# Tail keys read in place, weights fetched in odd units, first x tiles on another queue, pools that wait by tile

## Chip, cores, metric

The kernel runs on one core of one Trainium2 chip. The metric is the device time of one execution in microseconds (us). Before the change the median was 2362.5 us (3 runs, 2361.6 to 2363.9).

## The reference

Four layers in the order A, B, A, B on 2048 tokens of 640 numbers, each on the layer norm of its input, with a residual sum. (The norms and the sums are in the part that is cut here.)

```python
def _A_ref(x, wq, wk, wv, wo, beta):          # 32 heads of 20, 4 segments of 512 tokens
    ...
    for s in range(4):
        logits = einsum('bhqd,bhkd->bhqk', qs, ks) * scale + mask     # causal
        a_dot = softmax(logits) @ vs
        num, den = phi(qs) @ M, phi(qs) @ z + 1e-6                    # memory of earlier segments
        outs.append(g * num / den + (1 - g) * a_dot)
        M, z = M + phi(ks)^T vs, z + sum(phi(ks))
    return o @ wo

def _B_ref(x, mem0, Wq, Wk, Wv, Wo, seg_len): # 32 heads of 128, 64 steps of 32 tokens
    mem = mem0                                # 8 memory tokens
    for s in range(64):
        h = concatenate([mem, xs])            # 8 + 32 rows
        q, k, v = h Wq, h Wk, h Wv
        p = softmax(where(mask, q k^T * scale, -1e9))
        o = (p v) Wo
        mem = o[:8]                           # the next step needs it
        outs.append(o[8:])
```

## The kernel before

Layer A works in 32 units (4 segments times 8 groups of four heads). Each unit ends in one VectorE addition called `a_r`, so the distance from one `a_r` to the next is the time of a unit. Layer B does 64 dependent steps. Of a step's 32 tokens, 24 are put through with the 8 memory tokens; the last 8 (the "tail") of four steps are projected together in advance (`b_QTt`, `b_KTt`, `b_Vtb`) and each step takes its own 8 of them.

The first A layer also fetches the projection weights of B, 15 portions of 1 MB (four loads each), one per unit:

```python
xts = [ln_load(0, tt, "a_xt" if tt < 2 else "a_xr") for tt in range(4)]  # SyncE's queue (SP)
fill_pads = prep() if prep else None    # q and k weights of A, ScalarE's queue (ACT)
load_vo(A_wv)                           # a_wvo, 800 KB, SP
# ... cut
for u in range(NU + 1):
    if u + 2 < NU:
        wload(u + 2)                    # a_wt: two loads per unit
    if pre and u >= 1:
        pre.pop(0)()                    # 1 MB of B's weights
```

In B the tail's keys are copied into the step's key tile (GpSimd) and its values are loaded into another tile (DMA), so that the second score and value matmuls (`k = 1`) can use 8 columns or rows of them:

```python
def tails_to_seg(s):
    T, i = divmod(s, 4)
    nc.gpsimd.tensor_copy(heads(QT[s])[:, :, 32:40], QTt[T][:, :, 8 * i:8 * i + 8])
    nc.gpsimd.tensor_copy(heads(KT[s])[:, :, 32:40], KTt[T][:, :, 8 * i:8 * i + 8])
    for j in range(4):
        nc.sync.dma_start(Vt[s][32 * j:32 * j + 8, :, :],
                          Vtb[T][32 * j + 8 * i:32 * j + 8 * i + 8, :, :])
# ... cut: scores
for k, n in ((0, 32), (1, 8)):
    for j in range(4):
        nc.tensor.matmul(o, lhsT=KT[s][:, 40 * h + 32 * k:40 * h + 32 * k + n], ...)
```

The start of a B layer asks for its first x tile, for 5 MB of output weights, and for the second x tile. It builds the mask there too:

```python
ln_dma(0)                               # b_xt, 160 KB
nc.sync.dma_start(m0[:, 0, :], mem0)
for q in range(4):                      # b_wo, 4 x 1280 KB
    nc_raw.sync.dma_start(W.wo[:, 8 * q:8 * q + 8, :], wo_src[:, 8 * q:8 * q + 8, :])
ln_dma(1)                               # b_xt, the second
ln_norm(0); ln_apply(0); ln_tr(0)
# ... cut: b_blk and b_mask built; tails and first queries and keys
ln_norm(1); ln_apply(1)                 # waits for the second b_xt, on VectorE
```

Names in the profiles below: in A, `a_st` are the layer-norm statistics of an x tile, `a_VP` and `a_PP` are projections on TensorE and `a_KN` the keys transposed by it. In B, `b_Qa` is the first projection of a step's queries, `b_Kb` the last one of its keys, `b_TQ` their transposition on VectorE, and `b_OPSd` the output projection of the tails.

Memory of a pool that closes is given to the pools that open after it; by default the first users of that memory wait for all that the closed pool's users in the region had outstanding.

## Time and profile before

| what | before |
|---|---|
| median of 3 runs | 2362.5 us |
| TensorE (PE) busy | 2226.6 of 2364.3 us (94%) |
| four steady steps of B | 52.4 us |
| the two B layers, `b_Qa` to the last `b_OPSd` | about 1680 us |
| first A layer, first to last `a_r` | 266.4 us |
| second A layer, the same | 259.6 us |

Three lines of the profile's page of the kernel before. The second has each engine's busy time, its share of the span and its instructions. In the third each digit is a fortieth of the span: the busy share of the DMA engines in tenths.

```profile
span 2364.3 us, 123472 instructions
PE 2226.6 (94%) x54988; PEld 1242.1 (53%) x54988; DVE 1578.4 (67%) x3636; ACT 949.3 (40%) x2207; POOL 1073.2 (45%) x2603
DMA  6773341111111111110033333400000001000000
```

TensorE is busy for 94% of the span. The DMA engines are busy in the A layers and nearly idle in B. The first A layer (about five digits) starts with 67733: bunched.

The windows view of before. Columns: stretch (us), its length, then busy time of each engine with the number of instructions, granted clock (the share of full speed at which TensorE's clock ran), DMA share, GB/s.

```profile
core 0: us, PE busy (x) PEld busy (x) DVE busy (x) ACT busy (x) POOL busy (x), PEclk, DMA share, GB/s
96.00:144.00 48.00, 39.34 (x413) 20.53 (x412) 31.02 (x80) 28.23 (x41) 20.18 (x49) 0.89 0.96 235
442.92:495.34 52.42, 52.20 (x1534) 29.54 (x1534) 35.97 (x79) 16.74 (x51) 25.70 (x62) 1.00 0.11 25
```

In 96 to 144 us the DMA engines are at 0.96 and TensorE is idle 8.7 of 48 us. In the steady B stretch of the last line TensorE is busy 52.20 of 52.42 us at full clock: it waits for 0.22 us, so relieving another engine can gain next to nothing there.

The chain of waits of before between 85 and 142 us (start, length, what was waited for): the work that ended last was held up by transfers.

```profile
88.16 7.28 DMA a_wt<-a_wpad
...
106.39 4.55 DMA a_wt<-a_wpad
...
110.96 5.92 DMA a_xt<-in_A_x_dram
...
128.94 10.22 DMA a_xt<-in_A_x_dram
```

```profile
1491.44 0.89 DVE L85 BATCH_NORM_STATS2 b_ln_st<-b_xt 128x6 f32<-128x320 bf16 x2 [2.65 <-DMA xres<-a_xr]
...
1511.30 0.85 DVE L85 BATCH_NORM_STATS2 b_ln_st<-b_xt 128x6 f32<-128x320 bf16 x2
```

```profile
1510.36 1.27 PE L85 MATMUL b_Qa<-b_wq,b_hT 128*32 128x512 bf16 x20
...
1514.38 0.61 PE L85 MATMUL b_Kb<-b_wk,b_hT 128*32 128x512 bf16 x8 [0.59 <-DVE b_TQ L85]
```

B's first statistics at 1491.44 waited 2.65 us for a store of layer A. The second x tile is asked for behind the four b_wo loads; its statistics at 1511.30 show no wait, and b_Kb starts at 1514.38 after a wait of 0.59.

The start of before, all engines; in brackets stands the idle time of the engine before the instruction, and what ended it:

```profile
0.81 2.15 SPq L215 DMA_DIRECT2D a_xt<-in_A_x_dram  x4
...
1.32 0.55 ACTq L143 DMA_DIRECT2D b_wv<-in_A_wk_dram  x1
...
3.00 0.74 SPq L198 DMA_DIRECT2D a_wvo<-in_A_wv_dram  x1
...
7.03 0.89 DVE L85 BATCH_NORM_STATS2 a_st<-a_xt 128x6 f32<-128x320 bf16 x2 [1.36 <-DMA a_xt<-in_A_x_dram]
...
16.06 0.95 ACT L85 COPY b_wv<-b_wv 128x400 bf16<-128x400 bf16 x2
```

Three value groups in a row on TensorE in before, two of 8 rows and one of 32. Each group is four matmuls, on four separate 32-row strips of the array. The groups start 25 ns apart in the median, behind one that streams 40 columns and behind one that streams 16 alike:

```profile
1519.29 0.17 PE L85 MATMUL b_OTL<-b_PT,b_Vt 8*128 8x16 bf16 x4
1519.32 0.18 PE L85 MATMUL b_OTL<-b_PT,b_Vsb 32*128 32x40 bf16 x4
1519.34 0.17 PE L85 MATMUL b_OTL<-b_PT,b_Vt 8*128 8x16 bf16 x4
```

### The profile page before, as it was taken

The page shows a single profiled execution, that of the slowest core. Times are in us where ns is not written, and L with a number is a line of the kernel's source. Part 1 is how long each engine was busy: PE and PEld are TensorE (multiplying, and loading weights), DVE is VectorE, ACT ScalarE, POOL GpSimd, SP SyncE. Part 2 cuts the span into 40 slices and gives each one's busy share as a digit, 9 for nine tenths or more (in the row PEclk, how much of TensorE's full clock was granted, in tenths as well). Part 3 has the DMA queues.
Part 4 walks back from the last instruction along what each step waited for, and adds up shares of the span by engine and source line. Part 5 has one row for each costly group of instructions (what it writes and reads, how often), then busy time and mean ns, then how long its engine had stood idle before and what let it go on. Part 6 is the DMA issues. An engine that isn't in the chain of part 4 may idle for free.

```text
span 2364.3 us, 123472 instructions
## 1 busy us (share of the span) xinstructions
PE 2226.6 (94%) x54988; PEld 1242.1 (53%) x54988; DVE 1578.4 (67%) x3636; ACT 949.3 (40%) x2207; POOL 1073.2 (45%) x2603
## 2 busy tenths in 40 slices
PE   7989979999999999999879998799999999999997
PEld 3444435555555555555545444455555555555554
DVE  6677646666666666666667776466666666666665
ACT  5666723332323233323257767133232323332322
POOL 3344434454454444544323444345445445444442
PEclk9999989999999999999989999899999999999999
DMA  6773341111111111110033333400000001000000
GB/s 173 196 184 99 107 143 24 26 23 26 24 24 23 25 26 26 23 24 21 21 115 109 107 108 109 151 22 23 20 22 20 22 22 23 22 23 21 19 18 16
DMA packets 98847, 131.83 MB, mean 56 GB/s; under 512 B 20592, under 2 KB 84096, under 8 KB 96384
## 3 DMA queue, kind: packets, MB, share of 16 engines
q1 hardware_dynamic: 96992, 122.21, 19.1%
q8 instruction: 431, 7.06, 1.3%
q10 hardware_dynamic: 1312, 1.64, 0.2%
q14 instruction: 112, 0.92, 0.1%
HBM read 89.17 MB, written 26.21 MB: 49 GB/s over the span
## 4 chain that ended last, share of the span: by engine, by line
PE 79%; DVE 10%; ACT 4%; issue 2%; DMA 2%; POOL 1%; SPq 0%; DVEq 0%; POOLq 0%; ACTq 0%
PE b_OPS L85 13%; PE b_V L85 12%; PE b_tail L85 7%; PE b_Qa L85 7%; PE b_Kb L85 6%; PE b_Qb L85 6%; PE b_Ka L85 6%; PE b_SP L85 4%; PE a_PP L85 4%; PE b_OTL L85 3%; ACT a_PT L85 3%; PE b_OPSd L85 3%; PE a_S L85 2%; PE a_pv L85 2%; DVE b_TM L85 1%
## 5 line engine op out<-in xcount | busy, mean ns | idle before, releaser
L85 PEld LDWEIGHTS <-b_hT 128*32 128x32 bf16 x15520 | 379.9, 96 | 339.5 <-DVE b_hT L85 65.8
L85 ACT ACTIVATE b_PT<-b_SP 128x224 bf16<-128x224 f32 x256 | 92.2, 360 | 773.1 <-DVE b_TQ L85 731.1
L85 PE MATMUL b_V<-b_wv,b_hT 128*32 128x512 bf16 x5120 | 361.5, 381 | 0.0
L85 ACT ACTIVATE a_PT<-a_S 128x768 bf16<-128x768 f32 (+1 forms) x384 | 326.5, 892 | 67.4 <-PE a_S L85 57.0
L85 PE MATMUL b_OPS<-b_wo,b_OTsb 128*32 128x320 bf16 x8192 | 325.9, 300 | 5.9 <-DVE b_OTsb L85 5.1
L85 PEld LDWEIGHTS <-b_OTsb 128*32 128x32 bf16 x8192 | 195.1, 96 | 114.2 <-DVE b_OTsb L85 49.5
L85 POOL CAST b_QT<-b_TQ 128x384 bf16<-128x384 f32 x254 | 140.8, 554 | 238.5 <-DVE b_TQ L85 238.5
L85 ACT CAST b_OTsb<-b_OTL 128x320 bf16<-128x320 f32 x384 | 150.9, 428 | 228.3 <-PE b_OTL L85 200.3
L85 POOL CAST b_KT<-b_TQ 128x384 bf16<-128x384 f32 x254 | 142.5, 561 | 162.4 <-DVE b_TQ L85 161.2
L85 POOL TENSOR_TENSOR b_PT<-b_PT,b_R 128x64 bf16<-128x64 bf16 x256 | 105.1, 411 | 216.4 <-ACT b_R L85 191.9
L85 POOL TENSOR_SCALAR_AFFINE_SELECT a_PT<-a_PT 128x256 bf16<-128x256 bf16 x256 | 107.8, 422 | 199.3 <-ACT a_PT L85 188.1
L85 PE MATMUL b_Kb<-b_wk,b_hT 128*32 128x512 bf16 x2560 | 185.5, 381 | 1.2 <-DVE b_TQ L85 1.2
L85 PE MATMUL b_Qa<-b_wq,b_hT 128*32 128x512 bf16 x2560 | 161.7, 381 | 13.4 <-DVE b_hT L85 7.1
L85 PE MATMUL b_Qb<-b_wq,b_hT 128*32 128x512 bf16 x2560 | 160.4, 379 | 0.0
L85 PE MATMUL b_Ka<-b_wk,b_hT 128*32 128x512 bf16 x2560 | 160.4, 379 | 0.0
L85 PE MATMUL a_PP<-a_xnT,a_wt 128*128 128x512 bf16 x560 | 151.1, 404 | 7.5 <-DVE a_um L85 1.7
L85 PE MATMUL a_S<-a_qk 32*128 32x512 bf16 (+3 forms) x1024 | 138.8, 312 | 8.1 <-ACT a_PT L85 6.4
L85 DVE STREAM_TRANSPOSE b_TM<-b_OPS 128x320 f32<-128x320 f32 x126 | 65.2, 517 | 115.2 <-PE b_OPS L85 115.2
L85 DVE TENSOR_TENSOR b_PT<-b_PT,b_R 128x160 bf16<-128x160 bf16 x256 | 103.5, 404 | 49.4 <-ACT b_R L85 29.5
L85 DVE CAST b_Vsb<-b_V 128x512 bf16<-128x512 f32 x128 | 88.5, 692 | 68.2 <-PE b_SP L85 53.5
L85 DVE STREAM_TRANSPOSE b_TQ<-b_Qa 128x512 f32<-128x512 f32 x128 | 91.7, 716 | 62.5 <-PE b_Qa L85 40.9
L85 DVE CAST b_OTsb<-b_OTL 128x320 bf16<-128x320 f32 x128 | 62.9, 492 | 104.5 <-PE b_OTL L85 104.5
(148 smaller groups left out, 4154.9 us busy)
## 6 DMA issues: line engine op xcount, KB each, us to landing
a_wt<-a_wpad SPq DMA_DIRECT2D x112, 160.0 KB
b_wo<-in_B_Wo_dram SPq DMA_DIRECT2D x8, 1280.0 KB
b_Vt<-b_Vtb SPq DMA_DIRECT2D x512, 16.0 KB
b_XO<-xres SPq DMA_DIRECT2D x256, 30.0 KB
a_wvo<-in_A_wo_dram SPq DMA_DIRECT2D x8, 800.0 KB
b_wq<-in_B_Wq_dram SPq DMA_DIRECT2D x20, 256.0 KB
b_wk<-in_B_Wk_dram SPq DMA_DIRECT2D x20, 256.0 KB
xres<-a_xo SPq DMA_DIRECT2D x16, 320.0 KB
```

Of the source, the lines that this page charges most:

```text
L85: r = f(*a, **k)
```

## The change

1. The tail's keys and values are read where they lie. The second score and value matmuls use all 32 tail keys of the four steps; a mask per step hides 24 of them. The copies to `b_KT` and the `b_Vt` loads go. The masks are built once, in the first A layer ahead of the first `a_qk`, not at each start of B.
2. B's weights are fetched in odd units only, so the 15 MB are spread over twice as many units.
3. The first x tiles of each A layer are issued from ScalarE's queue.
4. All pools of A and B wait by tile: a tile in reused memory waits only for what used its own bytes.

The diff, cut to its core:

```diff
+def build_masks(nc, C):                          # called in the first layer A
+    C.mask = C.pool.tile([128, 4, 40], BF16, name="c_mask")
+    nc.vector.memset(C.mask[:], 0.0)
+    ...                                           # 16 affine_select on GpSimd
+    C.blk = C.pool.tile([128, 4, 32], BF16, name="c_blk")
+    ...                                           # 5 memsets on VectorE
-        st = ctx.enter_context(tc.tile_pool(name="a_state", bufs=1))
+        st = ctx.enter_context(tc.tile_pool(name="a_state", bufs=1, reuse_waits="tile"))
     ...                                           # likewise all pools of A and B
-        xts = [ln_load(0, tt, "a_xt" if tt < 2 else "a_xr") for tt in range(4)]
+        xts = [ln_load(0, tt, "a_xt" if tt < 2 else "a_xr", nc.scalar) for tt in range(4)]
-                if pre and u >= 1:
+                if pre and u % 2:
     ...
-            nc.gpsimd.tensor_copy(heads(KT[s])[:, :, 32:40], KTt[T][:, :, 8 * i:8 * i + 8])
-            for j in range(4):
-                nc.sync.dma_start(Vt[s][32 * j:32 * j + 8, :, :], Vtb[T][32 * j + 8 * i:32 * j + 8 * i + 8, :, :])
-        (b_blk, b_mask built at the start of B)
     ...
-                            nc.tensor.matmul(o, lhsT=KT[s][:, 40 * h + 32 * k:40 * h + 32 * k + n],
+                            nc.tensor.matmul(o, lhsT=KTt[T][:, h, :] if k else KT[s][:, 32 * h:32 * h + 32],
     ...
-                        V_ = Vsb if k == 0 else Vt[s]
+                        V_ = Vtb[T] if k else Vsb
```

More of the change, by code (lines that the diff above doesn't have):

```diff
@@ L103, in __getattr__ @@
         return getattr(self._nc, attr)
+def build_masks(nc, C):
+    if hasattr(C, "mask"):
+        return
+    C.mask = C.pool.tile([128, 4, 40], BF16, name="c_mask")
+    nc.vector.memset(C.mask[:], 0.0)
+    for j in range(4):
+        m = C.mask[32 * j:32 * j + 32]
+        nc.gpsimd.affine_select(out=m[:, :, 0:16], in_=m[:, :, 0:16], pattern=[[-8, 4], [0, 16]], compare_op=ALU.is_ge,
+                                fill=-1e9, base=0, channel_multiplier=1)
+        nc.gpsimd.affine_select(out=m[:, :, 0:8], in_=m[:, :, 0:8], pattern=[[8, 4], [0, 8]], compare_op=ALU.is_ge,
+                                fill=-1e9, base=7, channel_multiplier=-1)
+        nc.gpsimd.affine_select(out=m[:, :, 8:16], in_=m[:, :, 8:16], pattern=[[8, 4], [1, 8]], compare_op=ALU.is_ge,
+                                fill=-1e9, base=0, channel_multiplier=-1)
+        m = C.mask[32 * j:32 * j + 24, :, 16:40]
+        nc.gpsimd.affine_select(out=m, in_=m, pattern=[[0, 4], [1, 24]], compare_op=ALU.is_ge,
+                                fill=-1e9, base=0, channel_multiplier=-1)
+    C.blk = C.pool.tile([128, 4, 32], BF16, name="c_blk")
+    nc.vector.memset(C.blk[:], 0.0)
+    for j in range(4):
+        nc.vector.memset(C.blk[32 * j:32 * j + 32, j, :], 1.0)
 def watch(nc, C, sums, inverses):
@@ L180, in layer_A @@
     with ExitStack() as ctx:
-        st = ctx.enter_context(tc.tile_pool(name="a_state", bufs=1))
-        wk = ctx.enter_context(tc.tile_pool(name="a_wk", bufs=2))
-        wk1 = ctx.enter_context(tc.tile_pool(name="a_wk1", bufs=1))
-        pg = ctx.enter_context(tc.tile_pool(name="a_pg", bufs=2, space=PSUM))
-        pss = ctx.enter_context(tc.tile_pool(name="a_pss", bufs=2, space=PSUM))
-        ppv = ctx.enter_context(tc.tile_pool(name="a_ppv", bufs=1, space=PSUM))
+        st = ctx.enter_context(tc.tile_pool(name="a_state", bufs=1, reuse_waits="tile"))
+        wk = ctx.enter_context(tc.tile_pool(name="a_wk", bufs=2, reuse_waits="tile"))
+        wk1 = ctx.enter_context(tc.tile_pool(name="a_wk1", bufs=1, reuse_waits="tile"))
+        pg = ctx.enter_context(tc.tile_pool(name="a_pg", bufs=2, reuse_waits="tile", space=PSUM))
+        pss = ctx.enter_context(tc.tile_pool(name="a_pss", bufs=2, reuse_waits="tile", space=PSUM))
+        ppv = ctx.enter_context(tc.tile_pool(name="a_ppv", bufs=1, reuse_waits="tile", space=PSUM))
         MZ32 = st.tile([128, NG, 4, 21], F32, name="a_MZ32")
@@ L210, in wload, with ln_load @@
             wts[u] = [wt[:, 0], wt[:, 1]]
-        def ln_load(n, tt, tag="a_xt"):
+        def ln_load(n, tt, tag="a_xt", q=nc_raw.sync):
             r0 = n * 512 + tt * 128
             xt = wk.tile([128, D], xdt, name="a_xt", tag=tag)
-            nc_raw.sync.dma_start(xt[:], x_src[r0:r0 + 128, :])
+            q.dma_start(xt[:], x_src[r0:r0 + 128, :])
             return xt
@@ L283, in layer_A @@
         gg = W.gates(nc, st)
+        build_masks(nc, C)
         def run(gctx):
@@ L287, in run @@
             if general:
-                gp = gctx.enter_context(tc.tile_pool(name="a_gen", bufs=1))
+                gp = gctx.enter_context(tc.tile_pool(name="a_gen", bufs=1, reuse_waits="tile"))
                 negs = wk1.tile([128, 128], F32, name="a_negs", tag="a_xn")
@@ L594, in layer_B @@
     with ExitStack() as ctx:
-        st = ctx.enter_context(tc.tile_pool(name="b_state", bufs=1))
-        wk2 = ctx.enter_context(tc.tile_pool(name="b_wk2", bufs=2))
+        st = ctx.enter_context(tc.tile_pool(name="b_state", bufs=1, reuse_waits="tile"))
+        wk2 = ctx.enter_context(tc.tile_pool(name="b_wk2", bufs=2, reuse_waits="tile"))
         hp = qkp = sm = wk2
         wk = st
-        wop = ctx.enter_context(tc.tile_pool(name="b_wo", bufs=1))
+        wop = ctx.enter_context(tc.tile_pool(name="b_wo", bufs=1, reuse_waits="tile"))
         W.wo = wop.tile([128, 32, D], BF16, name="b_wo")
-        pp = ctx.enter_context(tc.tile_pool(name="b_ps", bufs=3, space=PSUM))
-        po = ctx.enter_context(tc.tile_pool(name="b_po", bufs=1, space=PSUM))
-        pot = ctx.enter_context(tc.tile_pool(name="b_pot", bufs=2, space=PSUM))
+        pp = ctx.enter_context(tc.tile_pool(name="b_ps", bufs=3, reuse_waits="tile", space=PSUM))
+        po = ctx.enter_context(tc.tile_pool(name="b_po", bufs=1, reuse_waits="tile", space=PSUM))
+        pot = ctx.enter_context(tc.tile_pool(name="b_pot", bufs=2, reuse_waits="tile", space=PSUM))
         def ps_tile(shape, dtype, name):
@@ L653, in heads @@
         def heads(t):
-            return t[:, 0:1280].rearrange("p (h c) -> p h c", c=40)
+            return t[:].rearrange("p (h c) -> p h c", h=32)
         def alloc_h(s):
@@ L665, in alloc_qk @@
             QT[s] = qkp.tile([128, 32 * 40], BF16, name="b_QT", tag="QT")
-            KT[s] = qkp.tile([128, 32 * 40], BF16, name="b_KT", tag="KT")
+            KT[s] = qkp.tile([128, 32 * 32], BF16, name="b_KT", tag="KT")
         def w_heads(Wt, c, b, j):
@@ L696, in place @@
             evac(eng, dst3[:, 16 * b:16 * b + 16, c0:c0 + (t1 - t0)], tq[:, :, t0:t1])
-        QTt, KTt, Vtb, Vt = {}, {}, {}, {}
+        QTt, KTt, Vtb = {}, {}, {}
         hx = {}
@@ L755, in tails_to_seg @@
             nc.gpsimd.tensor_copy(heads(QT[s])[:, :, 32:40], QTt[T][:, :, 8 * i:8 * i + 8])
-            nc.gpsimd.tensor_copy(heads(KT[s])[:, :, 32:40], KTt[T][:, :, 8 * i:8 * i + 8])
-            Vt[s] = qkp.tile([128, 2, 512], BF16, name="b_Vt", tag="Vt")
-            for j in range(4):
-                nc.sync.dma_start(Vt[s][32 * j:32 * j + 8, :, :], Vtb[T][32 * j + 8 * i:32 * j + 8 * i + 8, :, :])
         class OPass:
@@ L809, in layer_B @@
             nc.vector.memset(ones[:], 1.0)
-        blk = st.tile([128, 2, 4, 32], BF16, name="b_blk")
-        nc.vector.memset(blk[:], 0.0)
-        for j in range(4):
-            nc.vector.memset(blk[32 * j:32 * j + 32, 0, j, :], 1.0)
-            nc.vector.memset(blk[32 * j:32 * j + 8, 1, j, :], 1.0)
         if not general:
@@ L819, in layer_B @@
         nc.vector.memset(XO[:], 0.0)
-        negs = wk.tile([128, 32], F32, name="b_negs", tag="Vsb")
-        nc.vector.memset(negs[:], -1e9)
-        mask = st.tile([128, 40], BF16, name="b_mask")
-        maskf = wk.tile([128, 40], F32, name="b_maskf", tag="tsc")
-        nc.vector.memset(maskf[:], 0.0)
-        for j in range(4):
-            r0 = 32 * j
-            nc.gpsimd.affine_select(out=maskf[r0:r0 + 24, 16:40], in_=negs[r0:r0 + 24, 0:24],
-                                    pattern=[[-1, 24]], compare_op=ALU.is_gt, fill=0.0, base=0, channel_multiplier=1)
-            nc.gpsimd.affine_select(out=maskf[r0:r0 + 8, 8:16], in_=negs[r0:r0 + 8, 0:8],
-                                    pattern=[[-1, 8]], compare_op=ALU.is_gt, fill=0.0, base=0, channel_multiplier=1)
-        nc.vector.tensor_copy(mask[:], maskf[:])
         if general:
             maskq = st.tile([128, 40], BF16, name="b_maskq")
-            maskqf = wk.tile([128, 40], F32, name="b_maskqf", tag="tsc")
+            maskqf = wk.tile([128, 40], F32, name="b_maskqf", tag="xnb")
+            negs = wk.tile([128, 32], F32, name="b_negs", tag="Vsb")
+            nc.vector.memset(negs[:], -1e9)
             nc.vector.memset(maskqf[:], 0.0)
@@ L922, in row_max @@
                         h = 16 * b + 8 * q + i
-                        nc.tensor.matmul(sp[:, i, :], lhsT=QT[s][:, 40 * h:40 * h + 40], rhs=KT[s][:, 40 * h:40 * h + 40],
+                        nc.tensor.matmul(sp[:, i, 0:32], lhsT=QT[s][:, 40 * h:40 * h + 40], rhs=KT[s][:, 32 * h:32 * h + 32],
+                                         start=False, stop=True, skip_group_check=True)
+                        nc.tensor.matmul(sp[:, i, 32:40], lhsT=QT[s][:, 40 * h:40 * h + 40], rhs=KTt[T][:, h, 8 * i4:8 * i4 + 8],
                                          start=False, stop=True, skip_group_check=True)
@@ L965, in scores @@
                     nc.tensor.matmul(sp[32 * j:32 * j + 32, :, 0:40], lhsT=C.identb[:, 32 * j:32 * j + 32],
-                                     rhs=mask[:].unsqueeze(1).to_broadcast([128, 4, 40]),
+                                     rhs=C.mask[:, i4].unsqueeze(1).to_broadcast([128, 4, 40]),
                                      start=True, stop=False, tile_position=(0, 32 * j), skip_group_check=True)
                 for r in range(4):
-                    for k, n in ((0, 32), (1, 8)):
+                    for k in range(2):
                         for j in range(4):
                             h = 16 * b + 4 * j + r
-                            o = sp[32 * j:32 * j + n, r, 16:56] if k == 0 else sp[32 * j:32 * j + n, r, 0:16]
-                            nc.tensor.matmul(o, lhsT=KT[s][:, 40 * h + 32 * k:40 * h + 32 * k + n],
+                            o = sp[32 * j:32 * j + 32, r, 0:16] if k else sp[32 * j:32 * j + 32, r, 16:56]
+                            nc.tensor.matmul(o, lhsT=KTt[T][:, h, :] if k else KT[s][:, 32 * h:32 * h + 32],
                                              rhs=QT[s][:, 40 * h + 24 * k:40 * h + 40], start=False, stop=True,
@@ L976, in scores @@
                 if general:
-                    for k, n in ((0, 32), (1, 8)):
+                    for k in range(2):
                         for j in range(4):
                             h = 4 * j
-                            o = sp[32 * j:32 * j + n, :, 16:56] if k == 0 else sp[32 * j:32 * j + n, :, 0:16]
-                            nc.tensor.matmul(o, lhsT=ones[0:3, 0:n], rhs=mrows[b][:, h:h + 4, 24 * k:40],
+                            o = sp[32 * j:32 * j + 32, :, 0:16] if k else sp[32 * j:32 * j + 32, :, 16:56]
+                            nc.tensor.matmul(o, lhsT=ones[0:3, 0:32], rhs=mrows[b][:, h:h + 4, 24 * k:40],
                                              start=False, stop=True, tile_position=(0, 32 * j), skip_group_check=True)
@@ L990, in sums @@
                     for j in range(4):
-                        nc.tensor.matmul(sm_[32 * j:32 * j + 32, :, 24 * k:40], lhsT=blk[:, k, j],
+                        nc.tensor.matmul(sm_[32 * j:32 * j + 32, :, 24 * k:40], lhsT=C.blk[:, j],
                                          rhs=PT[:, b, :, 0:16] if k else PT[:, b, :, 16:56], start=(k == 0), stop=(k == 1),
@@ L1009, in values @@
                 for r in range(4):
-                    for k, n in ((0, 32), (1, 8)):
-                        V_ = Vsb if k == 0 else Vt[s]
+                    for k in range(2):
+                        V_ = Vtb[T] if k else Vsb
                         for j in range(4):
                             o = OTL[b, j // 2][:, j % 2, 40 * r + 24 * k:40 * r + 40]
-                            nc.tensor.matmul(o, lhsT=V_[32 * j:32 * j + n, b, 128 * r:128 * r + 128],
-                                             rhs=PT[32 * j:32 * j + n, b, r, 0:16] if k else PT[32 * j:32 * j + n, b, r, 16:56],
+                            nc.tensor.matmul(o, lhsT=V_[32 * j:32 * j + 32, b, 128 * r:128 * r + 128],
+                                             rhs=PT[32 * j:32 * j + 32, b, r, 0:16] if k else PT[32 * j:32 * j + 32, b, r, 16:56],
                                              start=(k == 0), stop=(k == 1), tile_position=(32 * j, 0))
@@ L1132, in layer_B @@
                 store_deferred(T, od)
-            hT.pop(s); QT.pop(s); KT.pop(s); Vt.pop(s)
+            hT.pop(s); QT.pop(s); KT.pop(s)
         if not general:
```

## The prediction

> **What bounds it now.** In steady B, TensorE. Busy time by stretch: 442.92-495.34 us (four steps, 52.42 us) has PE busy 52.20, granted clock 1.00, DMA share 0.11, VectorE 35.97, GpSimd 25.70. The two B layers are about 1670 of 2364 us. Then come two A layers, which mix PE with waits, and three layer changes where PE idles (timeline): 6.7 us before 320 (b_xn), 10.1 before 1188 (a_xn), 6.4 before 1494 (b_xn).
>
> **What the change does.**
>
> 1. Tail keys and values in place. Removes 128 GpSimd copies to b_KT (397 ns each, 50.8 us) and 512 small b_Vt loads, both off the chain: PE's waits over 345-1160 sum to about 4 us. In exchange the second score and value matmuls use 32 columns or rows instead of 8. Their count is unchanged; the 8-column weight load is 84 ns against 94 for 32, overlapped. Value groups of four start every 25-26 ns whether 40 or 16 columns stream[...]. Steady B should stay at 52.4 us per four steps; -0.5 us in all, from a copy less at each B start.
>
> 2. B's weights in odd units. In the first A layer the chain shows DMA waits at 88-95 (a_wt), 106-117 and 129-139 us (a_xt); DMA share is 0.96 in 96-144, PE busy only 39.3 of 48 us. From one a_r to the next, units 9-13 of the first A layer take 6.5 us more than those of the second, which fetches no such weights. Spreading the bytes should give most of it back: -5 us.
>
> 3. First x tiles on ScalarE's queue. The second x tile lands 1.4 us after VectorE wants it, beside two 800 KB loads; now x goes first. -1.5 us, but building masks on VectorE costs some 0.6 and the q/k weights land later: -0.7 us.
>
> 4. Waits by tile. Before, the first LayerNorm of B waits for the last a_xb copy and its store (b_ln_st at 317.43 and 1491.44, b_ln_rstd at 319.06 and 1493.07). By tile it needs only its own x; GpSimd still does the a_xb copies first (ending 317.32 and 1490.43), so rstd moves 1.7 and 2.6 us earlier: -4.3 us. At B-to-A the LayerNorm begins about 3 us earlier, but GpSimd's a_vaug fill, ahead of the rstd, still waits for the last b_XOd stores, which now queue behind three a_wt loads: only -0.7 us.
>
> **Sum.** -0.5 -5 -0.7 -4.3 -0.7 = about -11: 2351 us, 80% range 2344 to 2358. Faster by over 2%: 0.02; within 2%: 0.97; slower: 0.01.
>
> **What would show each step.** (1) GpSimd busy down about 45 us, b_Vt gone, four steps still 52.4 us. (2) DMA share near 0.5 in 50-150 us and up in 150-300; unit 13 at 9-10 us (before 13.75); no PE wait on a_xt or a_wt. (3) First transposes about 1.5 us earlier. (4) b_tail starts 2-3 us sooner after the last a_YP; the B-to-A idle of PE shrinks by 1-3 us at most.
>
> **What would make it wrong.** Wider weight loads slow the score groups (10 ns on each of 512 groups per layer is 5 us per layer). Late weights delay a_wvo or a_xt loads, or b_wv for B. Delayed q/k weights hold ScalarE at the start. The granted clock falls differently in A (0.88 against 0.94 in the last 50 us of the two A layers), some 3 us either way.

The "some 0.6" for the masks is an estimate; what before shows of such work is nine b_blk memsets on VectorE in 0.86 us (1494.30), and in after the six memsets of c_mask and c_blk took 0.73 us (26.46 to 27.19).

## More of the kernel before

The order of the transfers in the program is decided by a scheduler, which may move them past each other.

The passage from the second A layer to the second B layer in before: SyncE's queue (start, time to issue), VectorE, TensorE. In brackets stands the idle time of the engine before the instruction, and what ended it.

```profile
1492.29 6.37 SPq L800 DMA_DIRECT2D b_wo<-in_B_Wo_dram  x4
1498.76 4.84 SPq L625 DMA_DIRECT2D b_xt<-xres_bf  x1
```

## The result

| | median | range | runs |
|---|---|---|---|
| before | 2362.0 us | 2359.3 to 2363.9 | 4 |
| after | 2355.0 us | 2349.0 to 2357.2 | 4 |

Ratio 0.9967 (95% interval 0.9945 to 0.999): the same within 2%, some 7 us faster. A ratio is the mean time of one kernel's runs over that of the other's runs of the same rounds, so it is not quite the ratio of the medians. The predicted 2351 us was 4 us too low, within its range.

The page of after, the same lines as of before:

```profile
span 2351.1 us, 122636 instructions
PE 2217.0 (94%) x54988; PEld 1241.3 (53%) x54988; DVE 1576.1 (67%) x3618; ACT 949.9 (40%) x2207; POOL 1036.6 (44%) x2475
DMA  6555540000000000000124333300000000000000
```

The DMA row of the first A layer is now 65555, nearly flat. The two profiled spans differ by 13.2 us, nearly twice what the medians do, and the two granted clocks were 0.975 (before) and 0.981 (after). So part of the difference of these two profiles is luck, and a ledger from one pair would mislead. That is why the table further down uses fourteen profiles.

The windows view of after, the same columns (96 to 144 us, and four steady steps of B):

```profile
96.00:144.00 48.00, 43.05 (x506) 23.87 (x506) 38.24 (x96) 35.10 (x50) 23.52 (x55) 1.00 0.60 174
600.00:652.40 52.40, 52.17 (x1541) 29.54 (x1537) 35.92 (x79) 16.76 (x51) 24.48 (x58) 1.00 0.08 20
```

In 96 to 144 us the DMA share has fallen from 0.96 to 0.60 and TensorE is busy 43.05 us instead of 39.34. The chain of waits of after has no transfer between 40 and 300 us; before had the four above, 28.0 us in all. Four steady steps of B still take 52.4 us, with GpSimd a little less busy.

The second passage from A to B in after:

```profile
1476.10 6.63 SPq L819 DMA_DIRECT2D b_wo<-in_B_Wo_dram  x4
1482.83 4.61 SPq L649 DMA_DIRECT2D b_xt<-xres_bf  x1
```

```profile
1474.23 0.89 DVE L85 BATCH_NORM_STATS2 b_ln_st<-b_xt 128x6 f32<-128x320 bf16 x2 [1.60 <-DMA b_xt<-xres_bf]
...
1495.16 0.89 DVE L85 BATCH_NORM_STATS2 b_ln_st<-b_xt 128x6 f32<-128x320 bf16 x2 [2.27 <-DMA b_xt<-xres_bf]
```

```profile
1491.86 1.27 PE L85 MATMUL b_Qa<-b_wq,b_hT 128*32 128x512 bf16 x20
...
1498.27 0.61 PE L85 MATMUL b_Kb<-b_wk,b_hT 128*32 128x512 bf16 x8 [2.98 <-DVE b_TQ L85]
```

B's first statistics no longer wait for stores of A, and b_Qa comes 35.4 us after the last `a_r` (before 37.8). But the second x tile now lands after VectorE wants it (2.27 us of waiting at 1495.16). VectorE's transposition of b_Qa stands behind these statistics, and TensorE waits 2.98 us at b_Kb. From the first b_wo load (1476.10) to this b_Kb it is 22.17 us; before it was 22.09.

The start of after:

```profile
0.81 0.46 SPq L221 DMA_DIRECT2D a_wvo<-in_A_wv_dram  x1
0.84 1.98 ACTq L85 DMA_DIRECT2D a_xt<-in_A_x_dram  x4
...
1.89 8.92 SPq L606 DMA_DIRECT2D b_wq<-in_B_Wq_dram  x4
...
5.92 0.38 ACTq L166 DMA_DIRECT2D b_wv<-in_A_wk_dram  x1
...
8.98 0.89 DVE L85 BATCH_NORM_STATS2 a_st<-a_xt 128x6 f32<-128x320 bf16 x2 [3.06 <-DMA a_xt<-in_A_x_dram]
...
20.15 0.95 ACT L85 COPY b_wv<-b_wv 128x400 bf16<-128x400 bf16 x2 [2.51 <-DMA b_wv<-in_A_wk_dram]
```

The second x tile's statistics start 1.95 us later (8.98 against 7.03), and ScalarE waits until 20.15 us for the k weights, whose load was issued at 5.92 us instead of 1.32.

The value groups of after, TensorE. Those that stream 16 columns have 32 rows now and start at the same distances:

```profile
1504.48 0.17 PE L85 MATMUL b_OTL<-b_PT,b_Vtb 32*128 32x16 bf16 x4
1504.50 0.18 PE L85 MATMUL b_OTL<-b_PT,b_Vsb 32*128 32x40 bf16 x4
1504.53 0.17 PE L85 MATMUL b_OTL<-b_PT,b_Vtb 32*128 32x16 bf16 x4
```

One matmul group of the second A layer, the same place in the instruction order of before and after, TensorE:

```profile
1272.89 2.31 PE L85 MATMUL a_PP<-a_xnT,a_wt 128*128 128x512 bf16 x5
```

```profile
1259.67 1.25 PE L85 MATMUL a_PP<-a_xnT,a_wt 128*128 128x512 bf16 x5
```

The same five matmuls took 2.31 us in one profile, at a granted clock of 0.51, and 1.25 us in the other, at 1.00. So TensorE's clock dipped to half in before. Where such a dip falls differs from run to run of one program: in e8_after, which is after run again, a group of this kind took 2.32 us at 1291.96, and 1.24 us at its place in after (1290.43).

### The profile page after: what moved, and what is told of

The parts are those of the page before. It is cut to its first block, busy times and chain, and to the rows that moved or that the text cites. A ratio compares the mean times of both kernels' runs of the same rounds, so it can differ in the third digit from the quotient of the medians. Undisturbed runs are those within 1.5% of the kernel's fastest.

```text
span 2351.1 us, 122636 instructions
## 1 busy us (share of the span) xinstructions
PE 2217.0 (94%) x54988; PEld 1241.3 (53%) x54988; DVE 1576.1 (67%) x3618; ACT 949.9 (40%) x2207; POOL 1036.6 (44%) x2475
## 4 chain that ended last, share of the span: by engine, by line
PE 78%; DVE 10%; ACT 5%; DMA 3%; issue 2%; POOL 0%; SPq 0%; DVEq 0%; ACTq 0%; POOLq 0%
PE b_OPS L85 13%; PE b_V L85 13%; PE b_Qa L85 7%; PE b_tail L85 6%; PE b_Kb L85 6%; PE b_Qb L85 6%; PE b_Ka L85 6%; PE b_SP L85 4%; ACT a_PT L85 4%; PE a_PP L85 4%; PE b_OTL L85 3%; PE b_OPSd L85 3%; PE a_S L85 2%; PE a_pv L85 2%; DVE a_qk L85 2%
## 5 line engine op out<-in xcount | busy, mean ns | idle before, releaser
L85 PE MATMUL a_PP<-a_xnT,a_wt 128*128 128x512 bf16 x560 | 142.2, 385 | 6.7 <-ACT a_phiq L85 2.8
```

What stands on the lines that cost most here:

```text
L85: r = f(*a, **k)
```

## The experiments

Twelve runs, in the order in which they were made. The theory: the gain comes from relieved DMA in the first A layer and from the passages to B; the start lost by the change of queue; and the second passage's gain was given back. The rivals: half-clock dips (like the one at 0.51 above) that fell elsewhere, the building of masks, wider matmuls.

### e1_fetch: odd units alone

Before, with

```diff
-                if pre and u >= 1:
+                if pre and u % 2:
```

> The kernel before with one word changed: B's weights are fetched after odd units only. Theory (DMA relief): the loads no longer pile up on units 8 to 16 of the first A layer, so the TensorE waits on a_wt and a_xt there vanish; the first A layer from its first to its last a_r takes 258 us instead of 266 (after: 255.7), unit 13 (a_r to a_r) about 9.5 us instead of 13.75, DMA share near 0.5 in 96-144 us instead of 0.96, and the kernel is 6 to 9 us faster, about 2355. Rival (granted clock): what the first A layer gained in the changed kernel is half-rate dips of TensorE that fell elsewhere by luck; then this run gives 3 us or less, and the units that gain are not 9 to 13.

Measured: 2354.9 us median, before 2362.1 on the same chip, ratio 0.997 (0.995 to 0.999). From the first to the last `a_r` the first A layer took 257.5 us. This part alone is worth 7 us, as much as the whole change. Of the 8.8 us that the layer gained in the profile, 6.9 lie in units 9 to 13, most of it in unit 13 (8.85 us, before 13.74). The theory holds. The total alone doesn't exclude the rival's "3 us or less" (the interval allows a gain of 2.4 us); the stretch of units 9 to 13 in the table further down does.

### e2_xq: x tiles on ScalarE's queue alone

```diff
-        xts = [ln_load(0, tt, "a_xt" if tt < 2 else "a_xr") for tt in range(4)]
+        xts = [ln_load(0, tt, "a_xt" if tt < 2 else "a_xr", nc.scalar) for tt in range(4)]
```

> The kernel before with the first four x tiles of each A layer issued from ScalarE's queue, nothing else. Theory: this part alone makes the start later, because the 800 KB load of a_wvo and the weights of the second matrix now go ahead of or beside x and the q/k weights of A are issued some 4.6 us later; the first a_r comes 1.5 to 2.5 us later than 35.1, the second x tile's statistics start about 9.0 us instead of 7.0; the kernel is 1 to 2 us slower. Rival: the late start of the changed kernel is the building of masks on VectorE and GpSimd; then the first a_r stays at 35.1 or comes earlier (my prediction on record said 1.5 us earlier).

Measured: 2361.6 us, ratio 0.9997 (0.9978 to 1.0015). The first `a_r` came at 37.0 us, without any masks. The theory's size is right for the start. The second tile's statistics started at 6.6 us, not at 9.0; here it was the third that came late (9.67). The passage from B to A became longer as well: 39.7 us from the last b_OPSd to the first `a_r`, against 37.1. The total shows none of this loss: its interval allows 3.5 us more at most. In the profile, the second A layer was 3 us shorter than in that of before, without an edit that touches it.

### e3_waits: waits by tile alone

```diff
-        st = ctx.enter_context(tc.tile_pool(name="a_state", bufs=1))
+        st = ctx.enter_context(tc.tile_pool(name="a_state", bufs=1, reuse_waits="tile"))
(and so for the other pools)
```

> The kernel before with all pools of A and B waiting by tile, nothing else. Theory: the two passages from A to B shrink by 2 to 3 us each (last a_r to first b_Qa from 34.8 and 37.8 to about 32 and 35.5), the passage from B to A by under 1 us, and the start of the second B layer gives some 3 us back, because its second x tile is queued behind b_wo: in all -2 to -5 us. Rival: nothing is given back by this part (the 3.7 us that the second B layer lost has another cause, say x on ScalarE's queue or the clock): -5 to -7 us and B2 at 839.6 from first b_Qa to last b_OPSd.

Measured: 2364.6 us, ratio 1.001 (0.999 to 1.0031): nothing gained that can be seen in the total. The passages shrank to 32.9 and 36.0 us up to b_Qa. The second was partly given back at b_Kb, as the theory said, so that 40.6 us remain up to b_Kb (before 41.8). The expected -2 to -5 us did not show: this kernel's runs had the lowest mean clock of all kernels (0.9767). What it would have been at an equal clock stays within the noise.

### e4_tail: tail in place and masks alone

The first part of the diff above, the other three undone.

> The kernel before with the tail keys and values read in place and the masks per step, nothing else. Theory: steady B is bound by TensorE's columns and does not notice: 52.4 us per four steps, GpSimd's busy time 36 us less, the b_Vt loads gone; the masks cost 0.6 us at the first a_qk; in all between -1 and +1 us. Rival: the 32-column second weight loads and 32-row second value matmuls slow each step; then each B layer from first b_Qa to last b_OPSd takes 2 to 5 us more than 839.6, or fewer copies on GpSimd speed it up by as much.

Measured: 2359.4 us, ratio 0.9988 (0.997 to 1.0007). Of "TensorE's columns" the trace of before shows this: a projection matmul of 512 columns (b_Qb) has 62.7 ns of TensorE's busy time and one of 320 (b_OPS) 39.8 ns, but value groups start 25 ns apart behind 40 columns and behind 16. Steady B is not touched: from the first to the 63rd transposition of the memory tokens (b_TM) 814.1 and 813.3 us in the two B layers, before 813.4 and 813.3. From b_Qa to the last b_OPSd the layers took 840.2 and 843.0 us. The second number lies where the rival had it, but the excess is the wait at b_Kb shown below: from b_Kb on it is 836.6 us (before 835.6). By the medians this kernel is 2.7 us faster than before, more than the expected 1, though the interval of the ratio also allows no gain. The masks move the wait before the first a_KN from 0.79 to 1.25 us, so they cost 0.46 us. What I had not expected: the passages to b_Qa shrank to 32.9 and 35.4 us without any waits by tile. The instruction's waits in the trace say why: B's first statistics instruction has six waits in before (four DMA counters, ScalarE and GpSimd), but two in this kernel (one DMA counter and ScalarE); in the second B layer it is five and two. Leaving out tiles moved B's first tiles to other memory (that the placement is the reason is inferred, the shorter list of waits is not). And the second B layer's first b_Kb waited here, as in after:

```profile
1500.14 1.27 PE L85 MATMUL b_Qa<-b_wq,b_hT 128*32 128x512 bf16 x20
...
1506.55 0.62 PE L85 MATMUL b_Kb<-b_wk,b_hT 128*32 128x512 bf16 x8 [2.99 <-DVE b_TQ L85]
```

So what is given back in the second passage does not come from part 4, as I had supposed.

### e8_after: the changed kernel again

No edit.

> The changed kernel, not altered, once more: the base for the three other kernels of this call and a test of how much one profile varies. Theory: its time is again near 2355 us with a spread of some 8 us that goes with the granted clock (lower clock, longer run); the first a_r is near 37.3 us; the second B layer again waits some 3 us at its first b_Kb for a b_xt queued behind b_wo; but the 256.7 us of the second A layer was luck, and will be anywhere from 256 to 261. Rival: the second A layer's 256.7 belongs to the change and is repeated within 0.5 us.

Measured: 2356.1 us, before 2359.9 on this chip, ratio 0.998 (0.9962 to 0.9998). The second A layer took 259.1 us, against 256.7 in the first profile of the same program: that part was luck, and the rival falls. The start (37.6 us) and the wait at b_Kb repeat. The passage from B to A, 36.5 us in the first profile, was 34.3 here; that spread I can't explain. The time of the second A layer goes with its mean granted clock: 0.96 here and 0.97 in after, and over the fourteen profiles 0.94 in the longest (260.7 us), 0.96 in the five of 257.7 to 259.6 us, 0.97 or 0.98 in the eight of 255.9 to 257.4 us.

### e5_x_sp: part 3 undone

```diff
-        xts = [ln_load(0, tt, "a_xt" if tt < 2 else "a_xr", nc.scalar) for tt in range(4)]
+        xts = [ln_load(0, tt, "a_xt" if tt < 2 else "a_xr") for tt in range(4)]
```

> The changed kernel with the first x tiles back on SyncE's queue in both A layers. Theory (the queue made the start late): the first a_r comes at 33.5 to 34.5 us instead of 37.3; the passage from B to A stays at 36.5 within 0.5 us; 2 to 4 us faster than the changed kernel of the same call. Rival (the masks made it late): the first a_r stays above 36 us.

Measured: 2351.4 us, ratio to before 0.9959 (0.9939 to 0.9979), 4.7 us below the changed kernel of the same call by the medians, 3.8 by the means (expected 2 to 4). The first `a_r` came at 33.3 us. The queue made the start late, and the rival falls. The passage from B to A took 34.0 us, under the expected 36.5, but like that of e8. A by-catch: the stretch from the last b_OPSd to the end is 14.3 us here, and 15.7 to 16.3 us in every kernel that has both x on ScalarE's queue and the tail part, whereas e2 (only the first) has 14.5 and e4 (only the second) 14.4. The 1.5 us lie behind the last instruction of the flag (c_flag). The traces show where: in each of these six kernels SyncE pauses once, for 1.5 to 1.9 us, between two of its last semaphore instructions, and in no other kernel does it pause there for more than 0.43 us. The place of the pause is not the same in the six, so it is not one semaphore that is late; what causes it stays open.

### e6_xt1_first: the second x tile ahead of b_wo

The changed kernel with

```diff
+        ln_dma(1)
         for q in range(4):
             nc_raw.sync.dma_start(W.wo[:, 8 * q:8 * q + 8, :], wo_src[:, 8 * q:8 * q + 8, :])
-        ln_dma(1)
```

> The changed kernel with the load of the second x tile of each B layer issued ahead of the four b_wo loads. Theory: in before and in the changed kernel alike the second B layer's first b_Kb comes 22.1 us after the first b_wo load is issued, because the second x tile queues behind 5 MB; so what the second passage from A to B gained (last a_r to first b_Qa 37.8 to 35.4) was given back at the first b_Kb, and from the last a_r to that b_Kb both take 41.8. With x first that stretch is 38.5 to 39.7 us, b_Kb waits under 0.7 us, the second B layer from first b_Qa to last b_OPSd is back at 839 to 841, the first B layer as before: 2.5 to 3.5 us faster than the changed kernel. Rival (the 3.7 us that the second B layer lost are clock or the wider matmuls): nothing changes, 843.

Measured: 2353.0 us, 3.1 us below the changed kernel of the same call; ratio to before 0.9966 (0.9946 to 0.9986). From SyncE's queue and TensorE of this kernel:

```profile
1476.54 0.35 SPq L649 DMA_DIRECT2D b_xt<-xres_bf  x1
1477.06 7.74 SPq L820 DMA_DIRECT2D b_wo<-in_B_Wo_dram  x4
```

```profile
1491.67 1.27 PE L85 MATMUL b_Qa<-b_wq,b_hT 128*32 128x512 bf16 x20
...
1495.68 0.61 PE L85 MATMUL b_Kb<-b_wk,b_hT 128*32 128x512 bf16 x8 [0.59 <-DVE b_TQ L85]
```

The wait is back at 0.59 us, the distance from the last `a_r` to b_Kb is 39.35 us (the changed kernel of the same call 41.56), and from b_wo to b_Kb it is 18.6. The theory's mechanism holds. The second B layer from b_Qa to its last b_OPSd took 842.1 us, not 839 to 841; the part after b_Kb took 838.1, and that part ranges from 835.6 to 839.8 us over all fourteen profiles without a pattern.

### e7_all: both repairs, masks built later

e5 and e6 together, and `build_masks` cut into five pieces that run in units 2 to 6:

```diff
-        build_masks(nc, C)
+                if prep and 2 <= u < 8:
+                    build_masks(nc, C, u)          # a generator, one piece at each call
```

> Both repairs, and the masks built in five pieces during units 2 to 6 of the first A layer instead of ahead of the first a_qk. Theory: the savings add, 5 to 7 us faster than the changed kernel, about 2348 to 2350, with the first a_r at 33 to 34 us; it beats before by some 13 us. Rival: the stretches shorten but the clock of TensorE takes it back (more dips), and the gain is under 3 us.

Measured: 2350.3 us (2345.4 to 2355.1; the changed kernel of the same call 2354.5 to 2358.2), ratio to before 0.9957 (0.9936 to 0.9977), 5.8 us below the changed kernel. First `a_r` at 33.8 us, wait before the first a_KN 0.79 us again, the second passage 37.97 us to b_Kb (e5, which lacks the x repair: 40.28). The theory holds at its lower edge. This is the fastest kernel by its median; that it beats e5 (2351.4) is not shown by the totals, only by the stretches.

### e9_no_tile_waits: part 4 undone

The changed kernel with every `reuse_waits="tile"` taken out.

> The changed kernel with all pools waiting as they did before (waits by tile undone, the rest kept). Theory: the waits by tile are worth nothing on top of the tail part, because leaving out the second copies already moved B's first tiles off the memory whose stores they waited for; from the last a_r to the first b_Kb 36 to 37.5 us at the first passage and 41.5 to 42 at the second, as in the changed kernel; the time is within 2 us of the changed kernel's (about 2355 to 2356). Rival (my prediction on record): without them b_ln_st waits for the stores again and both passages are about 2 us longer: 38.5 to 39 and 43.5 to 44, some 4 us slower.

Measured: 2357.6 us, ratio to before 0.9982 (0.9965 to 0.9999). To b_Kb 37.3 and 40.75 us: no longer than with waits by tile. VectorE in the second passage:

```profile
1478.97 0.89 DVE L85 BATCH_NORM_STATS2 b_ln_st<-b_xt 128x6 f32<-128x320 bf16 x2 [1.81 <-DMA b_xt<-xres_bf]
```

It waits for its own x tile alone. So in the passages from A to B part 4 adds nothing to part 1, and the prediction falls in this step. At the passage from B to A it does matter: 40.6 us here, 34.3 to 36.8 in the five profiles that have waits by tile and x on ScalarE's queue. Without waits by tile, x on that queue is worse by 3 us (e2 too: 39.7) than x on SyncE's (36.5 to 37.2 in before, e1, e4, e10).

### e10_before_xt1: the repair of e6 on the kernel before

> The kernel before with the second x tile of B asked for ahead of b_wo (the scheduler lets one of the four b_wo loads stay in front of it in the second B layer). Theory: in before the tile landed just as VectorE became free for it, so nothing waited: last a_r to first b_Kb stays at 38.8 and 41.8 within 1 us, and the time stays within 2 us of before. Only the shorter passage of the changed kernel made this load the last to arrive. Rival (the load behind b_wo was binding already): the second stretch shrinks by 2 us or more.

Measured: 2362.6 us, ratio 1.0003 (0.999 to 1.0017); 37.9 and 41.75 us to b_Kb. Nothing gained, as the theory said. The load behind b_wo is worth moving only after the passage has been shortened.

### e11_swapped: q/k weights on SyncE's queue

The changed kernel with

```diff
-        nc.scalar.dma_start(raw[:, k], src.rearrange("(c p) n -> p c n", p=128))
+        nc.sync.dma_start(raw[:, k], src.rearrange("(c p) n -> p c n", p=128))
```

> The changed kernel with the q/k weights of A on SyncE's queue ahead of everything there; x stays on ScalarE's. The two queues have swapped, with the order that before had. Theory (what counts is which loads are issued first, not which engine issues them): the second x tile's statistics start at 6.3 to 7.3 us instead of 9.0, the q/k weights land by 15 us instead of 20, and the first a_r comes at 33.3 to 35 us; 2 to 4 us faster than the changed kernel. Rival (ScalarE's queue itself is slow for x): the first a_r stays at 36.5 to 37.5.

Measured: 2352.7 us, ratio to before 0.9958 (0.9943 to 0.9972). The total is as the theory had it, but its reason is not: the first `a_r` came at 36.6 us, inside the rival's range. The k weights were there by 17 us and no longer held ScalarE; the second x tile's statistics began at 7.72, the third's only at 10.19. One us of the three came back. By the ratios to before this kernel is 2 to 5 us better than the changed kernel, by its stretches one; it ran on another chip, and I have no account for the rest.

### e12_swapped_all: a_wvo on ScalarE's queue too

e11 with

```diff
-        load_vo(A_wv)
+        load_vo(A_wv, nc.scalar)
```

> The kernel of e11 with the first a_wvo load also on ScalarE's queue, behind the four x tiles. In e11 the q/k weights landed early again, yet the first a_r came at 36.6 us: the third x tile still landed after VectorE wanted it (10.2 us), with the 800 KB a_wvo load issued at 1.9 us on SyncE's queue, while x was being issued. Now the two queues hold what the other held in before, in the same order. Theory (any 800 KB load issued beside x delays x, whatever engine issues it): the fourth tile's statistics start by 10.5 us, as in before (10.2), and the first a_r comes at 33.5 to 35.3 us. Rival (x on ScalarE's queue comes late by itself): the first a_r stays at 36 us or more.

Measured: 2355.7 us, ratio to before 0.9968 (0.9941 to 0.9995; 4 runs). The start of this kernel:

```profile
3.36 0.47 ACTq L85 DMA_DIRECT2D a_wvo<-in_A_wv_dram  x1
...
10.81 0.88 DVE L85 BATCH_NORM_STATS2 a_st<-a_xt 128x6 f32<-128x320 bf16 x2
...
16.93 7.32 PE L85 MATMUL a_VP<-a_wvo,a_xnT 128*128 128x320 bf16 x35 [1.38 <-DMA a_wvo<-in_A_wv_dram]
```

The x tiles are nearly in time (fourth at 10.81, before 10.22; I had set 10.5). Now a_wvo is late, and TensorE waits for it at its first a_VP. The first `a_r` came at 37.15 us: the rival's number, though not because x is late. So which load comes last changed with the order of issue (k weights in after, awaited for 2.51 us; a_wvo here, for 1.38 us); that x issued from ScalarE's queue costs 3 us in every arrangement that I tried is shown, why the swap doesn't restore before's start is not. The swap was not complete either: SyncE's queue kept the load of beta (1.89 us) and the first of B's weights (6.11 us).

### All profiles together

One profile per kernel, in us. "Fetch stretch" runs from the 8th to the 13th `a_r` of the first A layer. "A1 to b_Kb" and "A2 to b_Kb" are from the last `a_r` of the layer to the first b_Kb of the B layer behind it. "B to A" runs from the start of the last group of b_OPSd to the first `a_r` of the second A layer.

| kernel | start to first `a_r` | A1 | fetch stretch | A1 to b_Kb | B to A | A2 | A2 to b_Kb |
|---|---|---|---|---|---|---|---|
| before | 35.1 | 266.4 | 52.3 | 38.8 | 37.1 | 259.6 | 41.8 |
| e1_fetch | 33.4 | 257.5 | 45.4 | 39.2 | 36.7 | 257.4 | 40.6 |
| e2_xq | 37.0 | 263.4 | 52.0 | 38.2 | 39.7 | 256.6 | 41.7 |
| e3_waits | 33.5 | 263.4 | 52.4 | 36.9 | 36.7 | 260.7 | 40.6 |
| e4_tail | 34.4 | 261.6 | 51.6 | 36.9 | 36.5 | 259.2 | 41.8 |
| e10_before_xt1 | 33.9 | 260.5 | 50.3 | 37.9 | 37.2 | 259.0 | 41.8 |
| after | 37.3 | 255.7 | 43.8 | 35.9 | 36.5 | 256.7 | 41.8 |
| e8_after | 37.6 | 253.8 | 45.3 | 37.2 | 34.3 | 259.1 | 41.6 |
| e9_no_tile_waits | 37.3 | 255.6 | 46.5 | 37.3 | 40.6 | 255.9 | 40.8 |
| e5_x_sp | 33.3 | 257.1 | 43.8 | 36.7 | 34.0 | 257.1 | 40.3 |
| e6_xt1_first | 37.0 | 256.3 | 45.2 | 37.2 | 35.0 | 256.2 | 39.4 |
| e7_all | 33.8 | 258.3 | 43.8 | 36.5 | 34.4 | 257.1 | 38.0 |
| e11_swapped | 36.6 | 256.5 | 44.5 | 35.7 | 36.0 | 256.8 | 41.9 |
| e12_swapped_all | 37.2 | 253.9 | 44.7 | 37.3 | 36.8 | 257.7 | 40.9 |

Averages over kernels that share a part give each part's worth with the luck of single profiles reduced:

- Start: x on SyncE's queue 33.9 (seven profiles), on ScalarE's, the rest as in the change, 37.2 (after, e2, e6, e8, e9): +3.3 us. About 0.2 of it is the masks, which more of the second group build at the start.
- First A layer: fetching from unit 1 on 263.1 (five), in odd units 256.1 (nine): -7.0 us, of which 6.9 in the fetch stretch (51.7 against 44.8; the two groups don't overlap). The clock doesn't account for it: the layer's mean granted clock was 0.96 in e2 (263.4 us) and also in e1, e6, e7, e9 and e11 (255.6 to 258.3).
- A1 to b_Kb: 38.5 with neither the tail part nor waits by tile (four), 36.8 with one or both (ten): -1.8 us before rounding.
- A2 to b_Kb, all of b_wo ahead of x: 41.4 with neither (three), 41.2 with one or both (eight): -0.2 us, so nothing. With x first 39.4 and 38.0.
- B to A: 36.9 (before, e1, e4, e10) against 35.7 (after, e6, e8, e11, e12): -1.1 us, with a spread as large as that.
- The end: +1.5 us.

The sum is 3.3 - 7.0 - 1.8 - 0.2 - 1.1 + 1.5 = -5.3 us. All ten runs of the changed kernel average 2355.3 us, the 38 runs of before that accompanied the experiments 2361.9: -6.6 us. The account closes to about 1 us. It leaves out the second A layer, which ran between 255.9 and 260.7 us in the fourteen profiles and fetches none of B's weights. The nine kernels that fetch in odd units average 257.1 us there and the other five 259.0; since the time goes with the clock (see e8), I count it as noise, but a part of up to 2 us isn't excluded. The rounds of different calls ran on different chips besides.

The noise goes with something that can be read. Among the 38 runs of before, the nine with a mean granted clock of 0.976 or less took 2366.4 us on average, the eight with 0.980 or more 2356.9 (correlation of time and clock -0.82). That the clock is the cause of the spread and not only its companion is not tested.

## Why the prediction was right and where it was wrong

The class and the range were right (2355.0 predicted 2351, range 2344 to 2358). The sum was right to 4 us partly because errors of both signs met.

1. **Tail in place: right.** "Steady B should stay at 52.4 us per four steps": it did. The wider second matmuls cost nothing: value groups start 25 ns apart in the median in both kernels, and from the first b_Kb of a layer to its last b_OPSd the nine profiles with this part average 836.4 and 837.5 us, the five without 836.5 and 836.9. GpSimd's busy time fell by 36.6 us (predicted 45), which bought nothing, since TensorE was never waiting for it. The -0.5 us was too small: this part also shortens the first passage by 1.9 us (e4), which the prediction had given to part 4.
2. **Odd units: mechanism right, size too small.** The term "-5 us" measured -7.0 over fourteen profiles (e1 alone: -7 us in the total). The waits on a_wt and a_xt went from the chain, and the DMA share fell to 0.60. I had read "6.5 us more than those of the second" and allowed only part of it to come back; all of it came.
3. **First x tiles: wrong sign.** The step that failed is "now x goes first. -1.5 us". On its own queue x goes first only on that queue. SyncE's queue, freed of x, issued a_wvo at 0.81 us and the first of B's weights at 1.89 (before 3.00 and 4.35), and the second x tile's statistics began at 8.98 instead of 7.03 us. That loads of the two queues hold each other up is inferred; e11 and e12 agree as far as x is concerned (second tile at 7.7 and 7.6 us with the weights moved, 9.0 without). In e2 it was the third tile that came late. The q/k weights, put behind x on ScalarE's queue, waited besides. Measured +3.3 us instead of -0.7, with some of the masks' 0.5 in it. The prediction's last paragraph named "delayed q/k weights hold ScalarE at the start" as a risk and gave it no number.
4. **Waits by tile: half wrong, and put down to the wrong part.** The term "-4.3 us" for the two passages from A to B measured -1.8 and -0.2. In the first passage either part 1 or part 4 is enough (e3, e4, e9). In the second the prediction followed the first LayerNorm only; the next arrival on that chain, the second x tile behind 5 MB of b_wo, had arrived just in time in before and became the bound. (In after it was usable 19.06 us after the first b_wo load was issued; an estimate from that for before is 1492.29 + 19.06 = 1511.35, and VectorE came to it at 1511.30.) The sign of it is a constant distance: from b_wo to b_Kb 22.1 us in before, 22.2 in after. e6 shows that moving this load gives 2.2 us back, e10 that it would have given nothing before.
5. **B to A: about right.** -0.7 predicted, -1.1 measured with as much spread. The queue of part 3 would have made it 3 us worse (e2, e9), and part 4 is what prevents that.
6. **Not foreseen:** 1.5 us more after the last step, in a pause of SyncE whose cause is open; and a pair of profiles 13.2 us apart where the kernels are 6.6 us apart.

## What to carry to other kernels

When a wait is taken away, look for the arrival that comes next on the same chain, and see how far behind it lies: a load that lands just in time today can be tomorrow's bound (the second x tile of B: no wait in before, 2.27 us in after), and a distance that is equal before and after (here from b_wo to b_Kb) gives it away. Moving a load to another issuing queue also moves forward what stood behind it on the old queue (here a_wvo from 3.00 to 0.81 us, the first of B's weights from 4.35 to 1.89), so list what each queue issues next, not only the load that was meant to win. Where runs differ by as much as the change is worth, compare the same stretch over several kernels that share a part rather than two profiles.

## What else the traces and runs show

- The four matmuls of a value group, each on its own 32-row strip of the array, mostly start 1 to 6 ns apart (3 ns in the median), in before and in after. What starts 25 or 26 ns apart are groups that follow each other, which use the same strips again; behind the first group of a run of eight it is mostly 38 to 40 ns.
- Dips of the clock also fall in the middle of a layer (0.51 at 1272.89 us in before). The second A layer took 255.9 to 260.7 us in fourteen profiles, and runs of before ranged from 2353.2 to 2369.5 us, with the mean granted clock between 0.973 and 0.982.
- A change of queue changes when loads are there: the same loads shared out differently between the two queues moved the second x tile's first use between 6.3 and 9.2 us and the first `a_r` between 33.3 and 37.6 us.
- A small load behind large ones: 160 KB asked for behind four loads of 1280 KB was used 19 us after the first of these was issued (1476.10 to 1495.16).
- Memory that is reused between pools: the first statistics of B had six waits in before, one in e3, two in e4 and three in e9, which goes with 1.8 us at one passage.
